# Four PSUM banks shared by scores and gated products, three for transposes, and transposes three steps behind the scores

## The chip, the cores and the metric

The kernel runs on one core of one Trainium2 chip. The metric is device time in microseconds (us); the time of a kernel is the median of its runs. The profile shows one execution. Engines are named as in the profile: PE is TensorE (PEld its weight loads), DVE is VectorE, ACT is ScalarE, POOL is GpSimd, and SP's queue issues the DMAs.

## What is computed

Three layers follow each other in float32: causal attention with a memory term, a gated layer, and a second gated layer.

```
scores = where(causal, -1e9, q @ k.T / sqrt(D))         # B, H, S, D = 4, 8, 576, 64
a = softmax(scores);  local = a @ v
mem = (phi(q) @ M_prev) / (phi(q) . z_prev + 1e-6)      # phi(x) = max(x, 0) + exp(min(x, 0))
x = sigmoid(beta) * mem + (1 - sigmoid(beta)) * local   # 2304 tokens x 512
x = (sigmoid(x @ w_gate) * (x @ w_val)) @ w_out         # width 1536
h = x @ w_in;  out = (h * clip(h + 3, 0, 6) / 6) @ w_out2   # width 2048
```

## The kernel before

**Phases.** `phase_a` does all of attention and, woven into it, half of the first gated layer (6 of its 12 slices of width) for six blocks of 312 tokens. `phase_b` does the rest of the first gated layer, `phase_c` the second. Matrix products of the two gated layers run as three passes of fp32r (`mm3`), on weights that `w_convert` rebuilds from 64-bit words with two ScalarE and seven VectorE instructions (L132 to L143). The 18 weights of `phase_a` come through two staging buffers.

**Visits and steps.** Attention goes in 32 visits, one for two heads and one range of the rows. Per batch there are four visits of range 0 (three steps, blocks 0 to 2 of the rows, score widths 64, 192, 320) and then four of range 1 (two steps, blocks 3 and 4, widths 448 and 576, the latter as 320 and 256). That makes 80 steps; 20 belong to one batch.

**One step** of the loop in `phase_a` (L455 to L490) issues, in this order: the scores of its block, one bank for each of two heads (`score_part`, L249; VectorE reads each bank with one instruction, L254, and writes it as weights P to SBUF); at most two banks of transposes (`transpose_bank`, up to four transposes L313 into one bank, which ScalarE copies to T, L316); a waiting `pv` (L339: T times the values, twelve or twenty matmuls, then a copy to SBUF and a store to `xd`); half of the step's share of gated products where a second pair of scores or a third bank of transposes is due, then these; exp of the block's weights (ScalarE, L271); after the last block of a visit the scaling of the weights (`normalize`, L300 on ScalarE, L302 on VectorE) and an entry in `tq`, with the step from which the visit's three or five transpose banks may run; the rest of the share of products; in the first step of a visit the loads of visit v + 2 (`load_visit`), in the second the preparation of visit v + 1 (`prep_phi`, L220 to L228); in two of three steps from step 6 on, one weight conversion. `pv` follows one step after the last bank of transposes.

**Products.** `moe_a` yields after every group of three matmuls; `FILL` says how many groups a step takes: 4 during the first block, then 9, 6, 9, 6, 6. A gate or value tile takes four groups, an output tile six, all into one bank, then read by ScalarE (gate L385, output L403) or VectorE (value L387). A block may start (`ready`) when the last `pv` of the row range that it needs was issued one step before (`done`, `LAG`), and its first product runs two steps after the load and split of its tokens (`moe_x`, L361 and L154/L155; `LEAD`).

**Order and buffers.** The order on PE is the one in which the loop issues (`manual_schedule` for PE, L452). The order on the other engines and on SP's queue is made by the framework's planner, from its own timeline. A tile takes a free buffer of its pool, or waits for the release of one. The eight PSUM banks are dealt out as 2 for scores (`ps_s`), 2 for transposes (`ps_t`), 1 for `pv` (`ps_v`), 3 for products (`ps_m`). In SBUF, P has two buffers, aux (q rows and values of a visit) three, qk two.

Of the kernel before, what the change touches and what calls it, by code (L numbers as in the profile page):

```python
# [8 lines left out]
F32 = mybir.dt.float32  # L9
# [6 lines left out]
PSUM = bass.MemoryType.PSUM  # L16
# [23 lines left out]
BANKS = [  # L40
    [_T[0][0:4], _T[0][4:8], _T[0][8:12]],
    [_T[1][4 * n : 4 * n + 4] for n in range(5)],
]
# [15 lines left out]
PW = [384, 640]  # L59
# [4 lines left out]
class Kernel:  # L64
# [99 lines left out]
    def open_attention(self, ctx):  # L164
        self.pa1 = self.pool(ctx, "pa1", 1)
        self.pa2 = self.pool(ctx, "pa2", 2)
        self.ps_s = self.pool(ctx, "ps_s", 2, space=PSUM)
        self.ps_t = self.pool(ctx, "ps_t", 2, space=PSUM)
        self.ps_v = self.pool(ctx, "ps_v", 1, space=PSUM)
        self.attn_consts(self.pa1)  # L170
        self.visits, self.done = {}, {}
# [59 lines left out]
    def score_part(self, v, i, a, e):  # L231

        nc = self.nc
        vs = self.visits[v]
        rg = 0 if i < 3 else 1
        n = i - RANGES[rg][0]
        nb = len(RANGES[rg])
        if n == 0 and a == 0:
            P = self.pa2.tile([128, 2, 2 * PW[1]], F32, name="P", tag="P")
            vs["P", rg] = P[:, :, : nb * PW[rg]].rearrange("p g (n c) -> p g n c", n=nb)  # L240
            vs["l", rg] = self.pa2.tile([128, 2, nb], F32, name=f"l{rg}", tag=f"l{rg}")
            vs["m", rg] = self.pa2.tile([128, 2, nb], F32, name=f"m{rg}", tag=f"m{rg}")
        P, m, qk = vs["P", rg], vs["m", rg], vs["qk"]
        q0 = QB[i][0]
        off = 448 if i == 0 else 512 - 128 * i
        tiles = []
        for g in range(2):
            rows = slice(64 * g, 64 * g + 64)
            ps = self.ps_s.tile([128, 512], F32, name="s", tag="s")  # L249
            nc.tensor.matmul(ps[:, : e - a], qk[rows, 0, q0 : q0 + 128], qk[rows, 1, a:e], start=True, stop=True)  # L250
            tiles.append(ps)
        for g, ps in enumerate(tiles):
            mm = m[:, g, n : n + 1]
            nc.vector.tensor_tensor_reduce(  # L254
                out=P[:, g, n, 64 + a : 64 + e],
                in0=ps[:, : e - a],
                in1=self.mask[:, off + a : off + e],
                scale=-0.125,
                scalar=3.0e38 if a == 0 else mm,
                op0=ALU.add,  # L260
                op1=ALU.min,
                accum_out=mm,
            )

    def exponentials(self, v, i):
# [3 lines left out]
        for g in range(2):  # L269
            x = vs["P", rg][:, g, n, 64 : 128 + 128 * i]  # L270
            self.nc.scalar.activation(  # L271
# [8 lines left out]
    def memory_rows(self, v, rg):  # L280

        pr = self.visits[v]
        i0, nb = RANGES[rg][0] - pr["j0"], len(RANGES[rg])
        out = pr["P", rg][:, :, :, 0:D]
        nr = pr["nr"][:, :, i0 : i0 + nb].unsqueeze(3).to_broadcast([128, 2, nb, D])
        self.nc.gpsimd.tensor_tensor(out, pr["ph"][:, :, i0 : i0 + nb, :], nr, op=ALU.mult)

    def normalize(self, v, rg, act):
        nc = self.nc
        pr = self.visits[v]  # L290
        h = pr["pair"][1]
        l, P, blk = pr["l", rg], pr["P", rg], RANGES[rg]
        a1 = self.a1[:, h : h + 2].unsqueeze(2).to_broadcast([128, 2, len(blk)])
# [53 lines left out]
    def open_moe_a(self, ctx):  # L347
        self.pm1 = self.pool(ctx, "pm1", 1, side="right")
        self.pm2 = self.pool(ctx, "pm2", 2, side="right")
        self.ps_m = self.pool(ctx, "ps_m", 3, space=PSUM, side="right")  # L350

    def ready(self, c):

# [53 lines left out]
    def phase_a(self):  # L407
# [11 lines left out]
        tq, vq = [], []  # L419

        def moe(k):
            nonlocal stream, c
            while k > 0:
                if stream is None:
                    if c == NCA:
                        return
                    if self.xnext is None or self.xnext[0] != c:
                        if not self.ready(c):
                            return
                        self.moe_x(c)  # L430
                    if self.step < self.xnext[2] + LEAD:
                        return
                    stream = self.moe_a(c)
                    c += 1
                try:
                    next(stream)
                    k -= 1
                except StopIteration:
                    stream = None

        def transposes(t, k):
            for _ in range(k):
                if tq and tq[0][0] <= t:
                    a = tq.pop(0)[1]
                    self.transpose_bank(*a)
                    if a[2] == len(BANKS[a[1]]) - 1:
                        vq.append((t + 1, a[:2]))

        t = self.step = 0
# [4 lines left out]
        while t < nt or tq or vq:  # L454
            self.step = t  # L455
            fill = FILL[max(c - 1, 0)]
            first = w = 0
            if t < nt:
                v, rg, i = steps[t]
                w = 64 + 128 * i  # L460
                first = w if w <= 512 else 320
                self.score_part(v, i, 0, first)
            if t == 0:
                self.prep_phi(0)
            if t < nt and i == RANGES[rg][1]:
                self.memory_rows(v, rg)
            transposes(t, 2)
            if vq and vq[0][0] <= t:
                self.pv(*vq.pop(0)[1])
            if first < w or (tq and tq[0][0] <= t):  # L470
                moe(fill // 2)
                fill -= fill // 2
                if first < w:
                    self.score_part(v, i, first, w)
                transposes(t, 1)
            if t < nt:
                self.exponentials(v, i)
                if i == RANGES[rg][-1]:
                    self.normalize(v, rg, 6 <= t < 34)
                    tq += [(t + 2, (v, rg, j)) for j in range(len(BANKS[rg]))]  # L480
            moe(fill)
            if t < nt and i == RANGES[rg][0]:
                self.load_visit(v + 2)
            if t < nt and i == RANGES[rg][0] + 1 and rg == VISITS[v][1][0]:
                self.prep_phi(v + 1)
            if t >= 6 and t % 3 < 2:
                self.w_convert()
            if len(self.wstaged) < 2:
                self.w_load()
            t += 1  # L490
# [4 lines left out]
        ctx = self.ctx  # L495
# [216 lines left out]
```

## Time and profile before

| | us |
|---|---|
| median of 3 runs | 1132.53 (1131.93 to 1133.65) |
| profiled execution | 1134.43 |
| its span, first to last instruction | 1132.7 |
| PE busy in the span | 1081.2 (95%) |
| DVE busy | 618.2 (55%) |
| ACT busy | 520.7 (46%) |
| mean granted PE clock | 0.976 |

A busy share over the whole span is a mean over stages: attention alone up to 86 us, attention with products up to about 440 us, then matrix products alone. Idle time before an instruction is given together with what ended it; `DVE m L254`, for example, is VectorE's read of a score tile. Product tiles are called `m` in the profile, score tiles `s`, transposes `t`; `m` on line 254 is the row minimum that this instruction also writes.

### The profile page before, as it was taken

The numbers are of one execution on the slowest core, as the hardware profiler recorded it, in microseconds if no ns is written. First come the engines' busy times: TensorE is split into PE (matmuls) and PEld (weight loads), VectorE is DVE, ScalarE is ACT, GpSimd is POOL, SyncE is SP. The second block draws the span as 40 slices with busy tenths as digits, with TensorE's granted clock in tenths as the row PEclk, the third lists the DMA queues.
The fourth block names the chain that finished last, engine by engine and source line by source line (L and its number), as shares of the span: only waits on it lengthen the run. The fifth ranks groups of instructions, "written<-read, shape, count | busy, mean of one in ns | idle before, by whom it ended". The sixth has DMA issues, their size and how long they took to land.

```text
span 1132.7 us, 16071 instructions
## 1 busy us (share of the span) xinstructions
PE 1081.2 (95%) x5984; PEld 927.1 (82%) x5984; DVE 618.2 (55%) x1589; ACT 520.7 (46%) x1179; POOL 56.5 (5%) x72
## 2 busy tenths in 40 slices
PE   5578899999999999999999999999999999999998
PEld 3346676887788769999888888989998998999997
DVE  7898745455445543999899328943223232322322
ACT  5686778555655564444443224423323242332322
POOL 2110210110011000000000000000000000000000
PEclk9677999999999999999999999999999999999999
DMA  5545334233223322534645306400101010010000
GB/s 190 159 136 169 99 106 120 80 115 100 87 61 115 93 69 103 181 112 130 192 146 161 102 14 196 152 4 7 50 1 56 1 56 1 1 56 1 28 1 28
DMA packets 57934, 98.53 MB, mean 87 GB/s; under 512 B 5376, under 2 KB 42240, under 8 KB 57856
## 3 DMA queue, kind: packets, MB, share of 16 engines
q1 hardware_dynamic: 57856, 97.51, 27.5%
q8 instruction: 47, 0.77, 0.3%
q14 instruction: 31, 0.25, 0.1%
HBM read 79.50 MB, written 17.99 MB: 86 GB/s over the span
## 4 chain that ended last, share of the span: by engine, by line
PE 85%; DVE 6%; DMA 5%; ACT 3%; issue 1%; SPq 0%; ACTq 0%; DVEq 0%
PE g L161 11%; PE g L159 11%; PE g L160 11%; PE acc L634 6%; PE acc L635 6%; PE acc L636 6%; PE m L159 5%; PE m L160 5%; PE m L161 5%; PE s L250 4%; PE t L313 4%; PE pv L339 4%; PE acc L159 3%; PE acc L161 3%; PE acc L160 3%; DMA wst<-in_wm 2%
## 5 line engine op out<-in xcount | busy, mean ns | idle before, releaser
L160 PE MATMUL g<-xs,wslot 128*128 128x384 f32 (+2 forms) x672 | 235.3, 351 | 0.0
L161 PE MATMUL g<-xs,wslot 128*128 128x384 f32 (+2 forms) x672 | 235.0, 351 | 0.0
L159 PE MATMUL g<-xs,wslot 128*128 128x384 f32 (+2 forms) x672 | 231.0, 351 | 0.0
L623 DVE SCALAR_TENSOR_TENSOR th<-th,g 128x384 f32<-128x384 f32 x96 | 53.0, 553 | 223.0 <-ACT th L622 222.7
L622 ACT ACTIVATE th<-g,three 128x384 f32<-128x384 f32 x96 | 55.8, 582 | 221.4 <-PE g L161 217.4
L160 PEld LDWEIGHTS g<-xs,wslot 128*128 128x128 f32 x672 | 126.1, 188 | 9.1
L159 PEld LDWEIGHTS g<-xs,wslot 128*128 128x128 f32 x672 | 126.0, 188 | 8.6
L161 PEld LDWEIGHTS g<-xs,wslot 128*128 128x128 f32 x672 | 126.1, 188 | 6.9
L250 PE MATMUL s<-qk 64*128 64x320 f32 (+4 forms) x384 | 89.3, 482 | 26.8 <-DVE m L254 22.3
L634 PE MATMUL acc<-wslot,hs 128*128 128x512 f32 x288 | 113.7, 395 | 0.0
L635 PE MATMUL acc<-wslot,hs 128*128 128x512 f32 x288 | 113.5, 394 | 0.0
L636 PE MATMUL acc<-wslot,hs 128*128 128x512 f32 x288 | 109.1, 393 | 0.0
L271 ACT ACTIVATE P<-P,m 128x64 f32<-128x64 f32 (+4 forms) x160 | 89.1, 558 | 37.3 <-DVE m L254 35.8
L155 DVE TENSOR_TENSOR hs<-th,hs 128x384 fp32r<-128x384 f32 (+2 forms) x132 | 76.0, 576 | 53.0 <-ACT hs L154 52.5
L154 ACT CAST hs<-th 128x384 fp32r<-128x384 f32 (+2 forms) x132 | 69.8, 529 | 76.2 <-DVE th L623 49.5
L313 PEld LDWEIGHTS t<-ident,P 128*128 128x128 f32 x480 | 57.7, 151 | 49.0 <-issue 20.0
L313 PE MATMUL t<-ident,P 128*128 128x128 f32 x480 | 78.2, 302 | 19.8 <-ACT T L316 8.7
L159 PE MATMUL m<-xs,wslot 128*128 128x312 f32 x288 | 94.8, 329 | 0.0
L160 PE MATMUL m<-xs,wslot 128*128 128x312 f32 x288 | 89.3, 310 | 0.0
L161 PE MATMUL m<-xs,wslot 128*128 128x312 f32 x288 | 88.8, 308 | 0.0
L250 PEld LDWEIGHTS s<-qk 64*128 64x128 f32 x384 | 38.6, 203 | 52.3 <-DVE m L254 33.3
L132 ACT ACTIVATE wf<-wst 128x512 f32<-128x512 f32 x68 | 46.0, 677 | 74.8 <-DMA wst<-in_wm 66.0
(74 smaller groups left out, 1810.7 us busy)
## 6 DMA issues: line engine op xcount, KB each, us to landing
wst<-in_wm SPq DMA_DIRECT2D x68, 512.0 KB, 3.6
aux<-in_aux SPq DMA_DIRECT2D x32, 192.0 KB, 3.1
qk<-in_qk SPq DMA_DIRECT2D x32, 160.0 KB, 2.5
aux<-in_aux SPq DMA_DIRECT2D x16, 320.0 KB, 4.0
qk<-in_qk SPq DMA_DIRECT2D x16, 288.0 KB, 3.0
x<-x SPq DMA_DIRECT2D x6, 768.0 KB, 4.5
out<-xp SPq DMA_DIRECT2D x18, 256.0 KB, 2.1
xc<-xd SPq DMA_DIRECT2D x6, 624.0 KB, 4.4
```

The costliest lines, as they stand in the source:

```text
L154: (ehi.copy if ehi is self.nc.scalar else ehi.tensor_copy)(hi, src)
L155: elo.tensor_tensor(lo, src, hi.bitcast(F32), op=ALU.subtract)
L159: nc.tensor.matmul(out, w[0], x[0], start=first, stop=False)
L160: nc.tensor.matmul(out, w[0], x[1], start=False, stop=False)
L161: nc.tensor.matmul(out, w[1], x[0], start=False, stop=last)
L250: nc.tensor.matmul(ps[:, : e - a], qk[rows, 0, q0 : q0 + 128], qk[rows, 1, a:e], start=True, stop=True)
L271: self.nc.scalar.activation(x, x, AF.Exp, bias=vs["m", rg][:, g, n : n + 1], scale=-1.0, accum_out=vs["l", rg][:, g, n : n + 1],)
L313: nc.tensor.transpose(ps[:, c : c + 128], src, self.ident)
L622: nc.scalar.activation(r[:, :CB], ps[:, :CB], AF.Relu, bias=self.three)
L634: nc.tensor.matmul(a, gs[:, 0, cc], w[:, 0, :], start=(f == 0), stop=False)
L635: nc.tensor.matmul(a, gs[:, 0, cc], w[:, 1, :], start=False, stop=False)
L636: nc.tensor.matmul(a, gs[:, 1, cc], w[:, 0, :], start=False, stop=(f == FF2 - 1))
```

## The change

Scores take their banks from the products' pool, under its tag, and that pool has four buffers. The transposes' pool has three. The pool `ps_s` is gone. P has three buffers. A visit's transposes may run from the third step after its last scores on, not from the second; `pv`, its store, `done` and the blocks of products move with them.

```diff
     def open_attention(self, ctx):
         self.pa1 = self.pool(ctx, "pa1", 1)
         self.pa2 = self.pool(ctx, "pa2", 2)
-        self.ps_s = self.pool(ctx, "ps_s", 2, space=PSUM)
-        self.ps_t = self.pool(ctx, "ps_t", 2, space=PSUM)
+        self.ps_t = self.pool(ctx, "ps_t", 3, space=PSUM)
         self.ps_v = self.pool(ctx, "ps_v", 1, space=PSUM)
...
         if n == 0 and a == 0:
-            P = self.pa2.tile([128, 2, 2 * PW[1]], F32, name="P", tag="P")
+            P = self.pa2.tile([128, 2, 2 * PW[1]], F32, name="P", tag="P", bufs=3)
...
-            ps = self.ps_s.tile([128, 512], F32, name="s", tag="s")
+            ps = self.ps_m.tile([128, 512], F32, name="s", tag="m")
...
-        self.ps_m = self.pool(ctx, "ps_m", 3, space=PSUM, side="right")
+
+        self.ps_m = self.pool(ctx, "ps_m", 4, space=PSUM, side="right")
...
                     self.normalize(v, rg, 6 <= t < 34)
-                    tq += [(t + 2, (v, rg, j)) for j in range(len(BANKS[rg]))]
+                    tq += [(t + 3, (v, rg, j)) for j in range(len(BANKS[rg]))]
```

## Rows read from the trace of the kernel before

**Rows 1.** Page: busy us of each engine, share of the span, instructions.

```profile
PE 1081.2 (95%) x5984; PEld 927.1 (82%) x5984; DVE 618.2 (55%) x1589; ACT 520.7 (46%) x1179; POOL 56.5 (5%) x72
```

**Rows 2.** Windows: length, busy PE, PEld, DVE, ACT, POOL, clock, DMA share, GB/s.

```profile
9.70:131.50 121.80, 89.21 (x434) 57.23 (x433) 111.03 (x318) 86.34 (x211) 18.71 (x19) 0.79 0.47 150
131.50:160.00 28.50, 26.51 (x191) 21.05 (x191) 13.67 (x58) 22.89 (x73) 6.02 (x7) 1.00 0.31 92
131.50:442.00 310.50, 302.87 (x2127) 245.99 (x2127) 152.50 (x581) 193.32 (x522) 35.75 (x45) 0.99 0.31 90
442.00:1132.70 690.70, 685.81 (x3417) 621.95 (x3415) 352.45 (x678) 237.39 (x437) 0.00 (x0) 1.00 0.23 73
```

**Rows 3.** Waits of PE, 0 to 131.5 us: us in total, times, longest.

```profile
PE s L250 <- DVE m L254: 21.1, 19, 4.3
PE t L313 <- issue: 5.4, 3, 2.3
PE t L313 <- DVE P L302: 4.6, 1, 4.6
...
PE t L313 <- ACT T L316: 2.3, 2, 2.0
PE t L313 <- ACT P L300: 1.0, 3, 0.3
```

**Rows 4.** Timeline of PE, step 13: start, us, instruction, [idle before, releaser].

```profile
55.42 2.31 PE L250 MATMUL s<-qk 64*128 64x320 f32 x4 [4.26 <-DVE m L254]
```

**Rows 5.** Timeline of DVE at the same place.

```profile
54.53 0.29 DVE L220 TENSOR_SCALAR phw<-aux 128x256 f32<-128x256 f32 x1 [2.08 <-DMA aux<-in_aux]
```

**Rows 6.** DVE groups, 9.7 to 131.5 us: count, busy us, mean ns, idle before.

```profile
L141 DVE SCALAR_TENSOR_TENSOR wst<-wst 128x512 f32<-128x512 uint32 x18 | 13.6, 755 | 0.2
L143 DVE TENSOR_TENSOR wslot<-wf,wslot 128x512 fp32r<-128x512 f32 x18 | 13.5, 751 | 0.0
L135 DVE SCALAR_TENSOR_TENSOR wf<-wst,wf 128x512 int32<-128x512 int32 x18 | 12.6, 700 | 0.1
L142 DVE TENSOR_TENSOR wf<-wf,wst 128x512 f32<-128x512 f32 x18 | 12.3, 683 | 0.3
L137 DVE TENSOR_SCALAR wst<-wf 128x512 int32<-128x512 int32 x18 | 8.6, 476 | 0.0
L133 DVE TENSOR_SCALAR wf<-wf 128x512 f32<-128x512 f32 x18 | 7.6, 420 | 2.8 <-ACT wf L132 2.7
L134 DVE TENSOR_SCALAR wf<-wf 128x512 int32<-128x512 int32 x18 | 7.5, 418 | 0.1
```

**Rows 7.** Waits of PE, 131.5 to 460 us.

```profile
PE t L313 <- ACT T L316: 6.4, 4, 2.6
PE s L250 <- DVE m L254: 1.2, 2, 0.8
```

**Rows 8.** Timeline of ACT at the start of the last block of products.

```profile
397.83 1.51 ACT L154 CAST xs<-xc 128x312 fp32r<-128x312 f32 x4 [3.41 <-DMA xc<-xd]
```

**Rows 9.** Timeline of PE there.

```profile
396.39 1.02 PE L250 MATMUL s<-qk 64*128 64x448 f32 x4
397.35 0.66 PE L313 MATMUL t<-ident,P 128*128 128x128 f32 x4
400.63 0.44 PE L313 MATMUL t<-ident,P 128*128 128x128 f32 x2 [2.63 <-ACT T L316]
```

**Rows 10.** Timeline of DVE there.

```profile
402.77 0.62 DVE L254 CUSTOM_DVE_ANT_0 P<-s,mask 128x448 f32<-128x448 f32 x1
```

**Rows 11.** Timeline of PE: the first product, two in a row, `pv` of step 23.

```profile
86.06 0.41 PE L159 MATMUL m<-xs,wslot 128*128 128x312 f32 x1
...
120.46 0.30 PE L161 MATMUL m<-xs,wslot 128*128 128x312 f32 x1
120.60 0.31 PE L159 MATMUL m<-xs,wslot 128*128 128x312 f32 x1
...
127.54 2.17 PE L339 MATMUL pv<-T,aux 128*64 128x256 f32 x20
```

## The prediction

> **What bounds the kernel now.** I read the page's busy times first, then the busy times by stage, then who waited for whom in each stage. Over the whole span TensorE is busy 1081.2 of 1132.7 us [rows 1], so all that any edit of buffers can win is its 51.5 us of idle time, plus time in which it ran at the low clock. The stages differ [rows 2]. From 442 us on TensorE idles 4.9 us in 690.7, most of it after its last matmul: nothing is to be won there. From 131.5 to 442 us it idles 310.5 - 302.87 = 7.6 us. From 9.7 to 131.5 us it idles 121.8 - 89.21 = 32.6 us, and the granted clock is 0.79, a mix of the two levels 1.2 and 2.4 GHz. In that stage VectorE is busy 111.03 of 121.8 us, 91%: it idles only 10.8 us, where TensorE idles 32.6.
>
> What TensorE waits for in the first 131.5 us: 21.1 us before score matmuls, until VectorE has read an older score tile out of its bank, and 13.3 us before transposes (5.4 without a named releaser, 4.6 for a weight that VectorE scales, 2.3 for a copy out of a transpose bank, 1.0 for a weight that ScalarE scales) [rows 3]. The longest single wait is 4.26 us before step 13's scores [rows 4]. There VectorE itself stood still 2.08 us for a load of aux before it reached the waiting score tiles [rows 5]. Elsewhere VectorE is at work, and most of its work is not attention: the seven lines of `w_convert` take 13.6 + 13.5 + 12.6 + 12.3 + 8.6 + 7.6 + 7.5 = 75.7 us for 18 conversions, 4.2 us each [rows 6]. These run ahead of their need. By the loop, twelve are issued in steps 6 to 22, and the products of steps 17 to 23 need seven; but all 18 are done when step 24 begins (131.5 us). After that VectorE is busy only 13.67 of 28.5 us [rows 2]. So in the first stage VectorE is full, and in part with work that could wait.
>
> After 131.5 us TensorE's waits are 6.4 us in four pieces before transposes, for ScalarE's copy out of a transpose bank, and 1.2 us before scores [rows 7]. The longest piece: ScalarE stood 3.41 us before the split of a new token block, whose load had not landed, and the next copy stood in its queue behind that split [rows 8]; the transposes that started at 397.35 had the other bank, and the next ones started at 400.63, 2.63 us late [rows 9].
>
> **The change, part by part.** No instruction is added or taken away; 192 score tiles, 128 transpose banks and 96 product tiles stay. Tiles of three kinds get other banks, and transposes and all that hangs on them move one step.
>
> Part A, the third transpose bank (after 131.5 us). At each of the four waits a visit's fourth or fifth bank of transposes needs a bank whose copy is queued on ScalarE. With three banks, and a group of three coming in the first step and two in the next, the late copy is a bank further away. If all four go: -6.4 us. What is late next is the score tile. In the same stretch the scores that started at 396.39 [rows 9] were read by VectorE only at 402.77, since VectorE was held by that split too [rows 10]. These two tiles, an open product and a product awaiting ScalarE make four, and the next score would wait. I price such a wait like the one that it replaces, 2.63 us, at three of the block starts: +7.9. So A lies between -6.4 and +1.5; I take -4, nearer the good end, because a full set of four tiles needs both engines late at once.
>
> Part B, scores with up to four banks and weights with three buffers (9.7 to 131.5 us). The 21.1 us of score waits are not the gain: VectorE has only 10.8 us of idle time there, and a wait that ends sooner in front of a busy engine comes back at the next instruction. A real gain needs VectorE to do less before step 24. The order of VectorE's queue is made by the planner from what is ready in its own timeline. When the next scores are written before the last are read, attention work is ready more often, and conversions move back. The room for them is the idle VectorE of 131.5 to 160 us: 28.5 - 13.67 = 14.8 us [rows 2], three conversions, 3 x 4.2 = 12.6 us. The other end: the aux buffer of visit v + 2 is free only after `pv` of visit v - 1, which comes one step later; behind its load on SP's queue stand weight and qk loads, and on VectorE the scores. Two more waits of 2.08 us [rows 5] would cost 4.2 us. So B lies between -12.6 and +4.2; I take half of the good end, -6. The third buffer of weights takes over what the longer way would otherwise block (`score_part` of a visit would wait for transposes of two visits before); it has no term of its own, since without it the longer way would not run.
>
> Part C, one step more between scores and transposes. It gives exp and scaling a step more, which is what the 4.6, 2.3 and 1.0 us waits of [rows 3] want; that gain is inside B, since VectorE bounds it. The cost: `done`, hence the start of each of the six blocks, comes one step later (the first product in step 18, not 17). If scores stay coupled to VectorE as now, TensorE has one step less done of everything else when VectorE gets free at 131.5 us. Step 23 holds one `pv`, 2.17 us, and twelve product matmuls that follow each other at 120.60 - 120.46 = 0.14 us, 1.7 us [rows 11]: 3.9 us that then run uncovered. If four banks let TensorE run one step further ahead, nothing is lost. So C lies between 0 and +3.9; I take +2. At the end nothing changes: 39 groups of three product matmuls still follow the last `pv`, some 17 us, under which the next phase's banks and weights come free (that phase now gets exactly the four banks that attention leaves, not four of five).
>
> Sum: -4 - 6 + 2 = -8 us. The profiled execution took 1134.43 us (span 1132.7 and 1.7 around it), so it would take 1126.4; the median of the runs, 1132.53, is 1.9 us under the profiled one, and I forecast 1132.5 - 8 = 1124.5 us, 0.7% faster.
>
> A rule weighed here. The Trainium skill, Perfetto Trace Analysis, Optimization Strategy, says that gaps repeating on the engine that should be saturated can mean too little PSUM for the next tile. By that rule alone the score and bank waits, 21.1 + 2.3 + 6.4 = 29.8 us, would all go, and the sum would be about 1103 us. The trace agrees that the wait is for a bank, but VectorE at 91% in the same stretch [rows 2] speaks against the size.
>
> **The rivals.** R1, the waits only change their name: VectorE keeps its order, the products hold two of the four banks so that scores get two as before, and TensorE's wait moves from scores to transposes. B is 0, C is +2, and A is -2 because score waits take back part. Result 1132.5. For it: VectorE's 91%. Against: before 86.06 us there are no products [rows 11], and scores do have four banks.
>
> R2, slower: the shared banks take away the running ahead. Its place is steps 18 to 30, where VectorE reads scores late and each open product holds a bank; TensorE takes its hand-written order in turn, so a product behind a score that waits for a bank waits too, which today never happens (no product wait is among [rows 3] or [rows 7]). Then C costs its full 3.9 and A its bad end 1.5: 1132.5 + 5.4 = 1138. It decides from the point where three tiles of the four are unread when a score pair is due.
>
> R3, large: conversions spread over all idle VectorE time until 160 us, 10.8 + 14.8 = 25.6 us, and the first stage ends that much earlier: 1107 us. For it: the idle time follows directly upon the overfull stage. Against: the loads and two staging buffers pace conversions, and ScalarE is busy 86.34 of the 121.8 us. The same page and section of the Trainium skill has a rule for this case, that regimes with different busiest engines may gain by being interleaved; no run here shows it yet.
>
> **How the numbers follow.** Forecast (1119 to 1130): 0.56. R1: 0.18, of which 0.03 falls under the bound of 0.2%. R2: 0.16. R3: 0.10. About 0.2%, 2.3 us, is what a measurement of this kernel can tell from no change. Faster by more: 0.56 + 0.10 + 0.03 = 0.69; within: 0.15; slower: 0.16. The ends of the terms together give 1132.5 - 19 = 1113.5 and 1132.5 + 9.6 = 1142; the range takes the good end and a little of R3, and R2: 1112 to 1138, leaving out most of R3 and the last of the bad end.
>
> **What would show it right or wrong.** A: no transpose waits above 1 us after the first stage, and no score or product waits of their size at the block starts. B: TensorE's idle time in the first stage falls from 32.6 towards 25 us, and some of the 18 conversions stand later than step 24. If VectorE's idle time there stays near 10 us with all 18 still inside, R1 holds. C: first product near its 86.06 us or earlier although it is a step later; well after it means R2. Wrong altogether would be a difference that comes after 450 us.

## The result, and the profile after

The changed kernel takes 1121.21 us (median of 4 runs, 1120.05 to 1124.64), the kernel before 1133.09 us beside it: a ratio of 0.9889 with a 95% interval of 0.9848 to 0.9931, so 12 us or 1.1% faster. The forecast was 8 us. A second series of the same kernel, further down, gives 0.9868 (0.9851 to 0.9884). The profiled execution took 1121.96 us with a span of 1120.2, 12.5 us shorter than before.

The page's busy times of the changed kernel, with the instructions of each engine at the end (the counts are those of [rows 1]: nothing was added or taken away):

```profile
PE 1074.1 (96%) x5984; PEld 925.4 (83%) x5984; DVE 616.9 (55%) x1589; ACT 517.9 (46%) x1179; POOL 55.8 (5%) x72
```

The same stretches as in [rows 2] (length, busy time with count of PE, PEld, DVE, ACT and POOL, granted clock, DMA share, GB/s), changed kernel:

```profile
9.70:131.50 121.80, 96.82 (x579) 67.25 (x578) 113.19 (x352) 100.43 (x273) 23.55 (x25) 0.95 0.52 165
131.50:160.00 28.50, 22.91 (x111) 15.45 (x111) 17.05 (x53) 16.21 (x39) 2.25 (x3) 0.73 0.29 82
131.50:442.00 310.50, 300.42 (x2060) 245.85 (x2061) 157.36 (x567) 183.73 (x474) 30.55 (x39) 0.97 0.31 94
442.00:1120.20 678.20, 673.79 (x3335) 610.22 (x3333) 344.10 (x660) 230.38 (x424) 0.00 (x0) 1.00 0.21 70
```

In the first of them TensorE runs 579 instead of 434 matmul instructions (scores and transposes among them), and idles 121.8 - 96.82 = 25.0 us instead of 32.6. VectorE runs 352 instructions instead of 318 in the same time, and its idle time there falls from 10.8 to 8.6 us. The second stretch got worse: TensorE idles 5.6 us instead of 2.0, at a clock of 0.73 instead of 1.00. After the last product the kernels are alike: 675.3 us from there to the end in both.

TensorE's waits in the first 131.5 us, as in [rows 3] (us in total, times, longest):

```profile
PE pv L338 <- ACT T L315: 7.3, 7, 1.6
PE s L249 <- DMA qk<-in_qk: 6.6, 2, 4.3
PE t L312 <- issue: 5.7, 2, 5.4
PE t L312 <- POOL phw L223: 4.1, 1, 4.1
PE s L249 <- DVE m L253: 2.0, 5, 0.8
PE m L161 <- DVE wslot L143: 1.8, 1, 1.8
PE t L312 <- DVE P L301: 1.2, 3, 0.6
```

The waits for a score bank are down from 21.1 us in 19 pieces to 2.0 in five, that for a weight scaled by VectorE from 4.6 to 1.2. What is late next is another engine: `pv` waits for ScalarE's copies (7.3 us), which was not among TensorE's waits of [rows 3], and 5.4 us of one wait have no named releaser (below). New too are 4.1 us in which a transpose waits for GpSimd, and a second wait for a load of qk (6.6 us in two, 4.4 in one before); the second profile of the changed kernel, further down, has neither.

After 131.5 us, as in [rows 7]:

```profile
PE m L161 <- DVE wslot L143: 5.0, 3, 3.6
PE pv L338 <- ACT T L315: 1.9, 2, 1.6
PE t L312 <- ACT T L315: 1.8, 1, 1.8
PE m L159 <- ACT wslot L140: 1.1, 1, 1.1
PE s L249 <- ACT xp L403: 0.6, 1, 0.6
```

Four waits for a transpose bank have become one, of 1.8 us, at a block start (170.78 us). New are waits of product matmuls for weights whose conversion is not done: 5.0 + 1.1 us here and 1.8 in the list above, 7.9 us in all. The two longest, in the timeline of PE (start, us, instruction, idle before and its releaser), and ahead of them the first product of all:

```profile
73.01 0.41 PE L159 MATMUL m<-xs,wslot 128*128 128x312 f32 x1
...
129.53 0.41 PE L161 MATMUL m<-ha,wslot 128*128 128x312 f32 x1 [1.77 <-DVE wslot L143]
...
134.07 0.63 PE L161 MATMUL m<-ha,wslot 128*128 128x312 f32 x1 [3.60 <-DVE wslot L143]
```

The first product runs at 73.0 us, not at 86.06 [rows 11], although it is now of step 18, not 17. The block start of that product shows where the longest remaining pause comes from. ScalarE at 65.57 us (first fence) stands 2 us for the load of the tokens, with scalings and copies queued behind the split; TensorE's next transpose starts at 67.75 us (second fence). The profile names no releaser for that pause; the reading rests on the order in time, the split until 67.08 us, a scaling behind it, then the transpose:

```profile
65.57 1.51 ACT L154 CAST xs<-xc 128x312 fp32r<-128x312 f32 x4 [2.00 <-DMA xc<-xd]
```

```profile
67.75 0.44 PE L312 MATMUL t<-ident,P 128*128 128x128 f32 x1 [5.40 <-issue]
```

**Where the 12.5 us came from.** Let a step begin with its first score matmul on PE. Step 24 begins at 99.7 instead of 131.5 us, but that flatters: only 10 of the 18 conversions are done by then, 18 before. All 18 are done in both kernels by step 32, which begins at 145.5 instead of 161.6 us. Up to that point both have done the same VectorE work, and the busy times from the span's start to step 32 are the balance of the change. Before (first fence) and changed (second), columns as above:

```profile
0.00:161.60 161.60, 120.61 (x644) 81.70 (x644) 127.22 (x390) 114.27 (x298) 26.74 (x34) 0.84 0.46 145
```

```profile
0.00:145.50 145.50, 108.86 (x622) 75.67 (x622) 126.12 (x390) 111.36 (x300) 26.20 (x34) 0.91 0.51 160
```

VectorE runs the same 390 instructions in 126.1 instead of 127.2 us, and it idles 145.50 - 126.12 = 19.4 instead of 161.60 - 127.22 = 34.4 us. These 15.0 us of idle time and 1.1 us of work are the 16.1 us. This says where the time went, not yet why. From step 32 to the last product the changed kernel then takes 299.4 instead of 295.8 us: 3.6 us go back. 16.1 - 3.6 = 12.5.

### The profile page after: what moved, and what is told of

Its sections match the earlier page's. It is cut to its first block, busy times and chain, and to the rows that moved or that the text cites. A ratio compares the mean times of both kernels' runs of the same rounds, so it can differ in the third digit from the quotient of the medians.

```text
span 1120.2 us, 16105 instructions
## 1 busy us (share of the span) xinstructions
PE 1074.1 (96%) x5984; PEld 925.4 (83%) x5984; DVE 616.9 (55%) x1589; ACT 517.9 (46%) x1179; POOL 55.8 (5%) x72
## 4 chain that ended last, share of the span: by engine, by line
PE 84%; DVE 6%; ACT 5%; DMA 4%; issue 1%; SPq 0%; POOL 0%; ACTq 0%; DVEq 0%
PE g L161 11%; PE g L159 11%; PE g L160 11%; PE acc L634 6%; PE acc L635 6%; PE acc L636 6%; PE m L159 5%; PE m L161 4%; PE m L160 4%; PE pv L338 4%; PE s L249 4%; PE t L312 3%; PE acc L159 3%; PE acc L161 3%; PE acc L160 3%; DMA wst<-in_wm 2%
## 5 line engine op out<-in xcount | busy, mean ns | idle before, releaser
L160 PEld LDWEIGHTS g<-xs,wslot 128*128 128x128 f32 x672 | 126.1, 188 | 9.1
L161 PEld LDWEIGHTS g<-xs,wslot 128*128 128x128 f32 x672 | 126.1, 188 | 6.9
L636 PE MATMUL acc<-wslot,hs 128*128 128x512 f32 x288 | 109.1, 393 | 0.0
L312 PE MATMUL t<-ident,P 128*128 128x128 f32 x480 | 74.4, 293 | 14.7 <-issue 5.7
L249 PE MATMUL s<-qk 64*128 64x320 f32 (+4 forms) x384 | 78.6, 473 | 9.6 <-DMA qk<-in_qk 6.6
L253 DVE CUSTOM_DVE_ANT_0 P<-s,mask 128x320 f32<-128x320 f32 (+3 forms) x160 | 66.1, 428 | 29.0 <-PE s L249 28.7
```

What stands on the lines that cost most here:

```text
L160: nc.tensor.matmul(out, w[0], x[1], start=False, stop=False)
L161: nc.tensor.matmul(out, w[1], x[0], start=False, stop=last)
L253: nc.vector.tensor_tensor_reduce(out=P[:, g, n, 64 + a : 64 + e], in0=ps[:, : e - a], in1=self.mask[:, off + a : off + e], scale=-0.125, s ...
L312: nc.tensor.transpose(ps[:, c : c + 128], src, self.ident)
L636: nc.tensor.matmul(a, gs[:, 1, cc], w[:, 0, :], start=False, stop=(f == FF2 - 1))
```

## The experiments

In all of them a time is a median with the ratio to the kernel before on the same chip, and the interval of that ratio. "Step 32" is the start of that step in the profile, "work" and "idle" are VectorE's up to there, and "rest" is the time from step 32 to the last product.

### The longer way alone

Three buffers of weights and transposes three steps behind, with the banks of before.

```diff
-            P = self.pa2.tile([128, 2, 2 * PW[1]], F32, name="P", tag="P")
+            P = self.pa2.tile([128, 2, 2 * PW[1]], F32, name="P", tag="P", bufs=3)
-                    tq += [(t + 2, (v, rg, j)) for j in range(len(BANKS[rg]))]
+                    tq += [(t + 3, (v, rg, j)) for j in range(len(BANKS[rg]))]
```

> The kernel before with the longer way alone: transposes three steps behind, three buffers of weights, banks as before (2 scores, 2 transposes, 3 products). In the program as built, VectorE's queue has 16 of the 18 weight conversions ahead of the first score read of step 24; before has 18 there, the changed kernel 11. Theory T (the gain comes from conversions that move back in VectorE's queue, less one step of uncovered TensorE work, 3.9 us): 2 conversions of 4.2 us less 3.9, so about -4 us, 1127 to 1132 us. Rival L (the extra step itself wins, because exp and scaling get more time): 1119 to 1124 us.

Measured: 1142.70 us, 1.0062 (1.0040 to 1.0083): slower. Neither theory's time was met; both had expected a gain. Its busy times up to step 32, and TensorE's waits over the whole span:

```profile
0.00:156.00 156.00, 120.75 (x620) 79.06 (x620) 126.44 (x390) 110.57 (x295) 25.68 (x34) 0.84 0.48 148
```

```profile
PE t L313 <- ACT T L316: 20.7, 13, 4.6
PE s L250 <- DVE m L254: 14.3, 17, 2.8
...
PE t L313 <- DVE P L302: 0.7, 1, 0.7
```

Step 32 comes 5.6 us earlier, so VectorE does win some idle time (29.6 instead of 34.4 us), and the wait for a scaled weight is gone (0.7 us). But transposes now wait 20.7 us for a bank where it was 2.3 + 6.4 = 8.7 us before [rows 3, 7], and the rest takes 309.2 instead of 295.8 us.

### The banks alone

Four shared banks and a third for transposes, with two buffers of weights and two steps.

```diff
-            P = self.pa2.tile([128, 2, 2 * PW[1]], F32, name="P", tag="P", bufs=3)
+            P = self.pa2.tile([128, 2, 2 * PW[1]], F32, name="P", tag="P")
-                    tq += [(t + 3, (v, rg, j)) for j in range(len(BANKS[rg]))]
+                    tq += [(t + 2, (v, rg, j)) for j in range(len(BANKS[rg]))]
```

(against the changed kernel)

> The changed kernel with transposes two steps behind and two buffers of weights again: the banks alone (4 shared, 3 transposes). VectorE's queue has 18 conversions ahead of step 24, as before. Theory T: only the waits for transpose banks after the first stage go, -2 to -5 us: 1128 to 1131 us, with 18 conversions done at step 24. Rival S (TensorE's 21.1 us of waits for score banks were the loss, and four banks end them): 1112 to 1122 us.

Measured: 1136.68 us, 1.0009 (0.9992 to 1.0026): no difference, so neither theory's gain came. Busy times up to step 32, and the waits of TensorE:

```profile
0.00:160.80 160.80, 117.41 (x644) 79.19 (x644) 128.31 (x390) 113.47 (x298) 26.52 (x34) 0.82 0.46 145
```

```profile
PE t L312 <- issue: 18.0, 5, 6.5
PE t L312 <- DVE P L301: 11.1, 5, 7.3
PE s L249 <- DVE m L253: 6.8, 6, 2.7
```

Here score waits fall to 6.8 us, and transposes wait instead: 11.1 us for weights that VectorE has not scaled yet, and 18.0 us without a named releaser. VectorE idles 32.5 us. This is the first rival of the prediction in what it says of the waits (they move from scores to transposes), but for half of the change. So neither half has the gain: +7 and +1 us alone, -12 together.

### The change with two transpose banks

```diff
-        self.ps_t = self.pool(ctx, "ps_t", 3, space=PSUM)
+        self.ps_t = self.pool(ctx, "ps_t", 2, space=PSUM)
```

> The changed kernel with two transpose banks in place of three (one bank stays unused). VectorE's queue has 16 conversions ahead of step 24. Theory T: as the longer way alone, about 1127 to 1132 us, and waits for transpose banks at the block starts come back. Rival A (the third bank matters only at the block starts, about 4 us): 1123 to 1126 us.

Measured: 1131.09 us, 0.9961 (0.9944 to 0.9977): the time and the waits of Theory T, though not its reason, since the longer way alone lost. Busy times up to step 32, then TensorE's waits from 150 to 460 us:

```profile
0.00:146.70 146.70, 110.24 (x621) 76.25 (x622) 126.62 (x390) 109.86 (x295) 26.10 (x34) 0.86 0.49 158
```

```profile
PE t L312 <- ACT T L315: 9.3, 7, 2.6
PE pv L338 <- ACT T L315: 2.3, 2, 1.4
```

Step 32 begins 1.2 us later than in the changed kernel: the first stage hardly needs the third bank once scores have four, although transposes wait 18.3 us for a bank between 9.7 and 131.5 us (1.2 us in the changed kernel). The rest needs it: 305.7 us instead of 299.4, with seven waits for a bank (9.3 us) where the changed kernel has one (1.8 us). With three steps between scores and transposes, two banks are worse than they were with two steps (6.4 us in four pieces [rows 7]).

### Own banks for scores

Three steps, three transpose banks, scores on two banks of their own, and two for products.

```diff
+        self.ps_s = self.pool(ctx, "ps_s", 2, space=PSUM)
-            ps = self.ps_m.tile([128, 512], F32, name="s", tag="m")
+            ps = self.ps_s.tile([128, 512], F32, name="s", tag="s")
-        self.ps_m = self.pool(ctx, "ps_m", 4, space=PSUM, side="right")
+        self.ps_m = self.pool(ctx, "ps_m", 2, space=PSUM, side="right")
```

(against the changed kernel)

> The longer way with three buffers of weights and three transpose banks, but scores and products apart: two score banks as before, two product banks. It differs from the changed kernel in the sharing alone. Theory S2 (three things stop TensorE one after the other, the score bank, the unscaled weight, the transpose bank, and each must be eased): score waits of 10 us or more come back in the first stage, step 32 begins near 155 us (changed kernel 145.5, before 161.6), and the time is 1126 to 1134 us. Rival T3 (steps and transpose bank do it, the score banks add nothing): step 32 near 146 us, 1119 to 1124 us.

Measured: 1129.53 us, 0.9955 (0.9938 to 0.9971). Theory S2 had the time and the score waits (11.6 us in the first 131.5), Theory T3 had step 32: each was right in part. Busy times up to step 32, and the waits of TensorE over the whole span:

```profile
0.00:146.60 146.60, 122.69 (x622) 82.23 (x622) 126.66 (x389) 109.42 (x292) 26.19 (x34) 0.86 0.50 158
```

```profile
PE s L250 <- DVE m L254: 13.1, 18, 1.6
PE pv L339 <- ACT T L316: 6.7, 6, 2.6
...
PE m L159 <- ACT xp L403: 1.9, 1, 1.9
```

Step 32 is again at 146.6 us, with scores waiting 13.1 us in 18 pieces where the kernel before has 22.3 us in 21 over the whole span. So the longer way needs one relief beside it for the first stage, and either will do: a third transpose bank (here) or four score banks (the kernel above). The rest is 305.8 us: the wait of a product for `xp`, ScalarE's read of an output tile (1.9 us), is one that three or four shared banks don't have. That it makes up the whole 6.4 us over the changed kernel isn't shown. After the last product this kernel is 2.7 us shorter than the others (672.6 us).

### Conversions held back in the kernel before

One staging buffer for weights instead of two, nothing else. (The pool holds two tiles of a conversion, the raw words `wst` and the working copy `wf`, so there is one of each.)

```diff
-        self.stage = self.pool(att_ctx, "wstage", 2)
+        self.stage = self.pool(att_ctx, "wstage", 1)
```

> The kernel before, banks and steps untouched, with one staging buffer for the weights of the first phase in place of two. That holds conversions back: VectorE's queue has 9 of 18 ahead of step 24 (before 18, changed kernel 11). Theory T: the first stage gains as in the changed kernel or nearly so, without its loss of a step and without its gain at the block starts: 1118 to 1126 us. Rival S (banks are what wins) and common sense on buffers (a staging buffer less makes weights later): 1132 to 1145 us.

Measured: 1165.15 us, 1.0261 (1.0234 to 1.0288): much slower, and slower than either theory said. Its waits of TensorE, the first and the third of the list:

```profile
PE m L159 <- ACT wslot L140: 30.7, 7, 5.3
...
PE m L161 <- DVE wslot L143: 11.4, 9, 1.5
```

Step 24 begins at 107.5 us instead of 131.5, on the old banks and the old two steps, with eight conversions done instead of 18. So it is in large part the conversions that make attention slow before step 24; the kernel before with most of their VectorE work left out (next) begins it at 109.1 us. But moving them back is no gain by itself: products then wait 30.7 + 11.4 = 42 us for weights, and step 32 begins at 194.2 us. This is why the balance has to be drawn at step 32 and not at step 24.

### Most of the conversions left out

The seven VectorE instructions of a conversion cut to one, in the kernel before and in the changed one.

```diff
+        if key[0] == 1 and key[1] < NFA:
+            sl = pool.tile([128, 2, 512], F32R, name="wslot", tag="wslot")
+            nc.scalar.copy(sl[:, 0, :], w)
+            nc.vector.tensor_tensor(sl[:, 1, :], w, sl[:, 0, :].bitcast(F32), op=ALU.subtract)
+            self.w[key] = sl
+            return
```

> The kernel before without six of the seven VectorE instructions in each of the 18 conversions of the first phase (the weights of that phase are then not the reference's): 62 us of VectorE work less in the first stage, all else in place. Theory V (VectorE's load is what stretches the first stage): 15 to 30 us faster than before, ratio 0.974 to 0.987. Rival S (TensorE's chain of score bank, weight, transpose bank sets it, whatever VectorE has to do): under 8 us faster, ratio over 0.993.

> The changed kernel without the same six VectorE instructions in each conversion of the first phase. Theory V: with the load gone the change has little to win, within 4 us of the kernel before without them. Rival S: it keeps its gain over that kernel, 10 us or more.

Measured: 1112.13 us, 0.9787 (0.9767 to 0.9807), for the kernel before without them, and 1105.68 us, 0.9733 (0.9713 to 0.9753), for the changed one. The conversions' VectorE instructions are worth 24 us in the old arrangement, as Theory V said, and twice what the change wins. Without them the change still wins 6.4 us, about half of its 12. So about half of its gain hangs on the conversions, and half is there without them: neither theory had that to itself. The edit also makes each conversion shorter, and the changed kernel then has no wait for weights, so it takes away more than VectorE's load. Busy times up to step 32, before and changed, both without them:

```profile
0.00:138.00 138.00, 111.16 (x646) 76.65 (x646) 72.26 (x282) 110.86 (x298) 24.78 (x34) 0.90 0.55 170
0.00:128.90 128.90, 103.11 (x622) 73.16 (x622) 71.06 (x282) 108.15 (x294) 24.12 (x34) 0.92 0.56 179
```

VectorE has 55 us less to do here and idles 65.7 and 57.8 us, yet step 32 comes only 23.6 and 16.6 us sooner than with the conversions; and the change still brings it forward by 9.1 us, where VectorE is far from full. What carries that half of the gain isn't shown. TensorE's waits for score banks, 8.0 us before and 1.2 in the changed kernel, are in its favour; the waits of `pv` for ScalarE's copies go the other way (1.0 and 9.6 us).

### The blocks one step earlier

```diff
-LAG, LEAD = 1, 2
+LAG, LEAD = 0, 2
```

> The changed kernel with LAG 0 in place of 1: each block of products starts in the same step as in the kernel before, one step earlier than in the changed one. Theory C (the longer way costs one step of TensorE work that runs uncovered, 1.7 us of products and 2.2 of transposes and pv; the products' part can be had back): 2 to 4 us faster than the changed kernel, ratio to before about 0.985 to 0.987. Rival: the lost step had been hidden by the running ahead, no difference to the changed kernel (0.989), or slower because ScalarE then waits longer for a block's load.

This gives the products back the step that the longer way costs them. Measured: 1132.09 us, 0.9959 (0.9943 to 0.9975), 8 to 10 us worse than the changed kernel by the ratios: the last part of the rival (ScalarE waits longer for a block's load) is the one that came. A wait of this size is new; TensorE's waits, the second and the fourth of the list:

```profile
PE m L159 <- ACT xs L154: 8.4, 2, 4.4
...
PE m L161 <- DVE wslot L143: 4.3, 3, 2.4
```

The first product of a block now comes before its tokens are loaded and split (8.4 us in two pieces). The lost step can't be had back in this way.

### Conversions issued sooner

In the changed kernel, a conversion in every step from step 4 on, against the waits for weights at 129.53 and 134.07 us. This kernel ran a second time beside the changed kernel, unchanged, on one chip.

```diff
-            if t >= 6 and t % 3 < 2:
+            if t >= 4:
```

> The changed kernel with conversions issued in every step from step 4 on, in place of two of three steps from 6 on. VectorE's queue then has 16 conversions ahead of step 30's scores where the changed kernel has 14. Theory W (the 7.6 us that TensorE waits for converted weights at steps 30 and 31, and the low clock after it, are lost time): 4 to 10 us faster than the changed kernel, ratio to before 0.980 to 0.985. Rival V (VectorE is full until step 31, so conversions that move forward push scores back): no difference to the changed kernel, 0.987 to 0.991.

> The changed kernel with conversions issued in every step from step 4 on, beside the changed kernel itself. Theory W (waits for converted weights at steps 30 and 31 are lost time): 2 us or more faster than the changed kernel. Rival V (VectorE is full until step 32): within 1.5 us of it.

> The changed kernel once more, beside the others of this call: ratio to before 0.985 to 0.992 by both theories.

Measured: 1121.13 us, 0.9867 (0.9846 to 0.9888), then 1119.50 us, 0.9871 (0.9853 to 0.9889), and for the changed kernel beside it 1120.26 us, 0.9868 (0.9851 to 0.9884). The waits for weights fall from 7.9 to 5.3 us (first of the two), and nothing is won: the conversions that come sooner push attention back (step 24 begins at 103.7 instead of 99.7 us), and step 32 comes at 144.2 and 143.3 us, against 145.5 and 144.1 in the two profiles of the changed kernel. VectorE's work up to step 32 is much the same in them (127.2 and 126.1 us), as the rival said; that it alone sets that moment isn't shown, since VectorE still idles 17.0 and 19.4 us there.

### One addition of each conversion on GpSimd

```diff
-        nc.vector.tensor_tensor(w, w, lof, op=ALU.add)
+        eng = nc.gpsimd if key[0] == 1 and key[1] < NFA else nc.vector
+        eng.tensor_tensor(w, w, lof, op=ALU.add)
```

> The changed kernel with one of the seven VectorE instructions of each conversion in the first phase (the add of the low part, 18 times, 12.8 us in the first 131.5) on GpSimd. VectorE has done 126 to 128 us of work when step 32 begins in every kernel of this study. Theory V (VectorE's work plus its idle time sets that moment): step 32 begins 5 to 12 us earlier than in the changed kernel (145.5 and 144.1), ratio to before 0.976 to 0.984. Rival W (conversions get longer by the way over GpSimd and TensorE waits for weights): no gain, ratio 0.986 or more, with more than the 7 us of waits for weights of the changed kernel.

Measured: 1125.62 us, 0.9903 (0.9882 to 0.9923): 2 to 4 us worse than the changed kernel by the ratios of its two series, and no better in any case: the cheaper VectorE queue that the edit was to bring is not there, and so Theory V was not put to the test. Rival W's numbers came, with 10.2 + 0.9 us of waits for weights instead of 7.9. The profiled execution was the slowest of the seven (1130.97 us). Its busy times up to step 32 (columns as above):

```profile
0.00:151.80 151.80, 115.23 (x620) 79.40 (x620) 130.38 (x372) 112.19 (x300) 51.39 (x52) 0.87 0.50 154
```

VectorE has 18 instructions less (372, not 390) and is busy 4.3 us longer. Its groups in this kernel from 9.7 to 149 us (count, busy us and mean ns, idle before):

```profile
L144 DVE TENSOR_TENSOR wslot<-wf,wslot 128x512 fp32r<-128x512 f32 x18 | 14.7, 816 | 1.9 <-POOL wf L143 1.9
L141 DVE SCALAR_TENSOR_TENSOR wst<-wst 128x512 f32<-128x512 uint32 x18 | 14.3, 795 | 0.1
...
L133 DVE TENSOR_SCALAR wf<-wf 128x512 f32<-128x512 f32 x18 | 11.7, 650 | 0.4 <-ACT wf L132 0.4
...
L137 DVE TENSOR_SCALAR wst<-wf 128x512 int32<-128x512 int32 x18 | 8.2, 458 | 0.0
```

The same groups of the changed kernel (L143 there is L144 here):

```profile
L142 DVE TENSOR_TENSOR wf<-wf,wst 128x512 f32<-128x512 f32 x18 | 14.9, 827 | 0.9 <-ACT wslot L140 0.6
...
L141 DVE SCALAR_TENSOR_TENSOR wst<-wst 128x512 f32<-128x512 uint32 x18 | 12.3, 686 | 0.1
L143 DVE TENSOR_TENSOR wslot<-wf,wslot 128x512 fp32r<-128x512 f32 x18 | 12.2, 680 | 0.0
...
L137 DVE TENSOR_SCALAR wst<-wf 128x512 int32<-128x512 int32 x18 | 9.2, 513 | 0.1
...
L133 DVE TENSOR_SCALAR wf<-wf 128x512 f32<-128x512 f32 x18 | 7.4, 413 | 1.9 <-ACT wf L132 1.9
```

The 18 additions that left (14.9 us) are eaten by what stayed: +4.3 us on L133, +2.5 on the subtraction into `wslot`, +2.0 on L141, +1.1 each on L134 and L135, -1.0 on L137, and about 8 us more on instructions outside the conversion, such as those of `normalize` and `prep_phi`. The 72 score reads, for one, stay as they were (28.1 and 27.8 us). What makes an instruction longer is seen in one pair, VectorE's (first fence) and GpSimd's (second):

```profile
115.05 1.39 DVE L133 TENSOR_SCALAR wf<-wf 128x512 f32<-128x512 f32 x1
```

```profile
114.87 1.28 POOL L143 TENSOR_TENSOR wf<-wf,wst 128x512 f32<-128x512 f32 x1 [1.62 <-ACT P L300]
```

GpSimd's addition runs until 116.15 us, and VectorE's instruction, started under it, ends 0.29 us later. Its median in this kernel is 0.42 us.

### The kernels side by side

Read from the timelines of PE (steps) and the busy times of VectorE; the work is the same in the first seven, the idle time is not. The ratio is of all runs of a kernel, the other columns are of one execution each, which lay between 2.4 us under its median and 4.1 us over it (the banks alone); so differences of a few us between two rows say little.

| kernel | ratio | step 24 | step 32 | work | idle | rest |
|---|---|---|---|---|---|---|
| before | 1 | 131.5 | 161.6 | 127.2 | 34.4 | 295.8 |
| longer way alone | 1.0062 | 126.1 | 156.0 | 126.4 | 29.6 | 309.2 |
| banks alone | 1.0009 | 131.7 | 160.8 | 128.3 | 32.5 | 302.6 |
| changed, two transpose banks | 0.9961 | 116.2 | 146.7 | 126.6 | 20.1 | 305.7 |
| changed, own banks for scores | 0.9955 | 114.9 | 146.6 | 126.7 | 19.9 | 305.8 |
| changed | 0.9889 | 99.7 | 145.5 | 126.1 | 19.4 | 299.4 |
| changed, again | 0.9868 | 98.2 | 144.1 | 126.2 | 17.9 | 298.1 |
| before, most of the conversions left out | 0.9787 | 109.1 | 138.0 | 72.3 | 65.7 | 297.3 |
| changed, most of the conversions left out | 0.9733 | 100.2 | 128.9 | 71.1 | 57.8 | 298.2 |

Ahead of step 32, three stops follow one upon another: a score tile waits for a bank, a transpose for a scaled weight, the next transpose for a bank. The longer way takes away the second, and one more bank for either of the others then lets VectorE's queue fill. The longer way comes with the third buffer of weights P in every run; what that buffer would do alone, or with the banks and two steps, was not run. After step 32 VectorE is not the bound; there the longer way costs, and only the full change keeps most of what was won.

Apart from the two that leave most of the conversions out, no kernel was measurably faster than the changed one. Whether a cheaper conversion on VectorE itself would win some of the 15 us between it and the changed kernel without conversions (1121.21 - 1105.68) stays open.

## Why the prediction was right, and where it was not

**Sign and mechanism: right; the sum in part by luck.** The time lies in the range and 3.3 us under the forecast. The gain is in the first stage, by fewer waits there and conversions that move back, and nothing comes after the last product, as said. But the forecast had a gain after the first stage too (A), and there the kernel loses; and of its three terms B lies beyond its good end and C, in the profiled execution, beyond its bad end, so that their errors partly cancel in the sum. TensorE's idle time in the first stage went from 32.6 to 25.0 us, the value named as the direction; conversions stand later than step 24 (8 of 18); and the first product comes earlier though a step later. The first rival, that waits only change their name, is what the banks alone do; it fell for the whole change, where the wait that would have followed is gone (transposes for weights that VectorE scales: 11.1 us with the banks alone, 1.2 with the longer way too).

**Term B was mis-sized: -6, bounds -12.6 to +4.2; measured -16.1 by the balance at step 32 (-17.5 in the second profile).** Two steps of the argument failed. The bound let VectorE keep its 10.8 us of idle time in the first stage and gave it only three conversions to move. In fact eight moved behind step 24, and what counts is not where they stand (with two transpose banks 15 are done at step 24, in the changed kernel 10, and step 32 comes within 1.2 us), but how much of VectorE's idle time up to step 32 is used. That is the pool of the third rival. It was 34.4 us, counted from the span's start, and the change used 15.0 of it. And the forecast took half of the good end without a row that spoke for a half. The bad end, more waits for aux, did not come. And the argument makes VectorE's queue the whole cause, while about half of the gain is there without most of the conversions' VectorE work.

**What stopped the third rival** (-25.6 us) on its way isn't shown. Product matmuls that need late weights wait 7.9 us in all, but the kernel with 5.3 us of such waits is no faster; `pv` and transposes wait for ScalarE's copies and splits, which no run eased. The rule weighed with that rival (the Trainium skill, Perfetto Trace Analysis, Optimization Strategy: regimes with different busiest engines may gain by being interleaved) is borne out in kind: VectorE's idle time until step 32 fell from 34.4 to 19.4 us, and conversions are among what was interleaved. That the attainable part would be 15 us could not be read from the rule. The other rule of that section weighed in the prediction, too little PSUM, gave about 1103 us; the banks alone measured 1136.68. It names a cause that is needed (the longer way without a bank more lost) and not enough.

**Term A: -4 forecast, bounds -6.4 to +1.5.** Against the kernel before, TensorE's idle time from step 32 to the last product fell only from 6.1 to 5.0 us (6.2 in the second profile): three of four waits for a transpose bank are gone (6.4 to 1.8 us), but `pv` waits 1.9 us in the same stretch. As a part of the change the third bank is worth more: 305.7 - 299.4 = 6.3 us, the good end, since with three steps two banks would have been worse than before. The step that failed was to price the bank against the kernel before, while another part of the change raises the need for it. Its sign of being right, no transpose wait above 1 us, was missed by one wait of 1.8 us. Score waits of 2.63 us at the block starts, its bad end, did not come; the largest is 0.6 us.

**Term C: +2 forecast, bounds 0 to +3.9.** By step 32, 168 product matmuls are issued instead of 180, so twelve and one `pv` run later: 1.7 us and at most 2.17 us [rows 11]. The rest grew by 3.6 us, of which A took off 1.0; so C measured +4.6 us, over its bound. It is all TensorE's busy time. From step 32 to the end of the last product, before (first line) and changed (second; columns as in [rows 2]):

```profile
161.60:457.90 296.30, 290.23 (x2031) 238.65 (x2031) 150.57 (x547) 177.70 (x463) 29.73 (x38) 0.99 0.32 96
145.50:445.40 299.90, 294.87 (x2055) 242.88 (x2055) 150.09 (x547) 178.12 (x460) 29.64 (x38) 0.99 0.31 95
```

The work that runs later accounts for up to 3.9 of the 4.6 us, as forecast, and the granted clock is 0.99 in both. The 0.97 of the changed kernel from 131.5 to 442 us comes mostly from before its step 32 (0.50 from 131.5 to 145.5 us). The forecast counted on TensorE running ahead for half of the deferred step, and here it had next to none of that. In the second profile of the changed kernel, where the clock after step 32 is 1.00, C is +2.2 us, near the forecast; with two executions its size stays open.

**A term that the sum did not have** is a product's wait for its weights, 7.9 us. The second rival looked for product waits in the right steps, 18 to 30, but for a bank; they came in steps 30 and 31, for a conversion that had moved back too far. They cost little in the end, since the kernel with 5.3 us of them is no faster.

## What to carry to other kernels

Where one engine is full in a stage and idle in the next, count its work up to the point where all kernels have done the same work, and its idle time up to there: as long as the work stays, that idle time is the most that an edit of buffers can win there (here 15.0 of 34.4 us came). The waits of the engines that depend on it say only where the queue stops: 18.3 us of waits for a transpose bank cost 1.2 us at step 32. Stops that follow each other have to be eased together; each of the halves here gave nothing or lost, and the whole gave 1.1%. To call one engine the bound, take its work away and see: here that gave 16.6 us for 55 us of work. And price each part of a change against the changed kernel too: a part can pay for what another one costs.

## What the runs showed of the hardware

**A VectorE instruction that starts under one of GpSimd can wait for its end.** With 25 us of additions moved to GpSimd (its busy time until step 32 rises from 26.2 to 51.4 us), VectorE's L133 went from 413 to 650 ns in the mean, L143/L144 from 680 to 816, L141 from 686 to 795, while L137 went from 513 to 458. The medians hardly moved: L133 417 and 420 ns, L137 422 and 419, L141 686 and 684, L143/L144 682 and 682. So the means are made by a few long instructions. Up to step 32, 11 of the 126 conversion instructions on VectorE are more than 60 ns over their usual time in the changed kernel, and 20 of 108 with the additions on GpSimd, 5.8 and 13.0 us in all; each of the 31 overlaps an instruction of GpSimd and ends after it. L137 isn't spared: it was hit three times in the changed kernel (719 to 1119 ns) and once here (1112 ns). The reads of score tiles, whose input is in PSUM, are not longer under GpSimd: 128x320 takes 477 ns in the mean beside it (9 of 24) and 477 ns otherwise. The Trainium skill, SBUF — State Buffer, Who interferes with whom, says that VectorE's second pair of ports is shared with GpSimd under an exclusive lock, so that of two instructions that need it one waits for the other's whole instruction. The pairs in this trace agree with that.

**Idle time and a low clock stand for each other.** The changed kernel and the one with own banks for scores reach step 32 within 1.1 us of each other, the one with a granted clock of 0.91 and 145.50 - 108.86 = 36.6 us of idle TensorE, the other with 0.86 and 146.60 - 122.69 = 23.9 us. Where another engine sets the pace, less idle time on TensorE is no gain: the same matmuls, partly at 1.2 GHz, fill it. So the 7.1 us by which TensorE's busy time fell in the changed kernel are best read not as a term beside the 16.1 us at step 32, but as another view of them.
